# Thirteen more short fills on VectorE at the beginning of a channel-attention kernel

## The chip, the cores and the metric

The kernel runs on 1 core of one Trainium2 chip. Times are device microseconds of that core for one execution, medians of several executions. Before the change the time was 743.05 us (three runs, 742.87 to 743.95).

## The reference

The input `x` is one image of 384 x 384 positions with 384 channels (bf16); `w1` is 384 x 96, `w2` is 96 x 384.

```python
def reference(x, w1, w2):
    B, H, W, C = x.shape
    xf = x.reshape(B, H * W, C)
    gap = jnp.mean(xf, 1)                  # mean of every channel
    gmp = jnp.amax(xf, 1)                  # maximum of every channel
    h_a = gap @ w1;  h_a = h_a * (h_a > 0)
    h_m = gmp @ w1;  h_m = h_m * (h_m > 0)
    scale = _sigmoid(h_a @ w2 + h_m @ w2)
    return x * scale[:, None, None, :]     # (dtype casts cut)
```

No output can be written before all of `x` has been read once. The kernel keeps part of `x` and reads the rest a second time: the page shows 198.92 MB read, and `x` has 113.25 MB.

## The kernel before

There are three stages. (1) All rows are loaded; TensorE sums them with a vector of ones, VectorE keeps a running maximum in `acc` (11 rows per partition). (2) A short serial stretch, called *the gate* below: the maximum is folded to one row, transposed, reduced, passed through the two small matrices and the sigmoid. (3) Every row is multiplied by the scale and stored, while the rows that had to be dropped are loaded again.

Setup, which the change touches:

```python
    small = consts.tile([P, 16], BF16)
    ones_bf = small[:, 0:1]
    # ... cut: other views of `small`; none of them covers column 9
    nc.vector.memset(ones_bf, 1.0)
    pick = small[0:NQP, 10:10 + 2 * CQ].bitcast(F32)
    nc.vector.memset(pick, 0.0)
    for q in range(CQ):                                   # CQ = 3
        nc.vector.memset(pick[q * QP:q * QP + 1, q:q + 1], 1.0)
    # ... cut
    nc.vector.memset(bank_a, 0.0)                         # 128 x 512 f32 in PSUM
```

`bank_a` is a tile that the program places in PSUM; in the trace TensorE's 900 matmuls of the sums write it (L143, `bank_a<-x,small`).

The load loop of stage 1 and the fold at the start of the gate (line numbers in the profile: copy into `acc` L179, maximum L183, fold L203, reduce L214, multiply L226):

```python
    for i, (first, n, s, lo, hi) in enumerate(loads):
        rows = slots[s][:, lo:hi, :]
        # ... cut
        nc.sync.dma_start(out=rows[:, a:b, :], in_=...)   # the first load in two parts
        # ... cut: sums on TensorE
        if i == 0:
            nc.vector.tensor_copy(out=acc, in_=rows[:, 0:A, :])
        for j in range(0 if i else A, m, A):
            nc.vector.tensor_tensor(out=acc[:, 0:k, :], in0=acc[:, 0:k, :], in1=rows[:, j:j + k, :], op=ALU.max)
        # ... cut: two copies that keep rows in PSUM
    # ... cut
    while n > 1:                                          # fold, n starts at A = 11
        h = n // 2
        nc.vector.tensor_tensor(out=acc[:, 0:h, :], in0=acc[:, 0:h, :], in1=acc[:, n - h:n, :], op=ALU.max)
        n -= h
```

A tile scheduler decides the order in which each engine gets its instructions, so an instruction need not stand where the program has it (the fill of L115 starts at 1.00 us, those of L95 at 1.48 us).

## Time and profile before

| what | before |
|---|---|
| time, median | 743.05 us |
| moved by DMA | 312.32 MB, 421 GB/s over the span |
| VectorE (DVE) busy | 489.4 us, 66% of the span |
| VectorE idle ahead of its first copy | 5.44 us |
| gate, first fold step to first multiply | 5.50 us |

The page of the kernel before: span, busy time by engine, the DMA's busy share in 40 slices of the span in tenths, GB/s in the same slices, and the two queues that carry instructions (packets, MB, share of 16 engines).

```profile
span 741.5 us, 2477 instructions
PE 127.2 (17%) x966; PEld 40.6 (5%) x966; DVE 489.4 (66%) x168; ACT 3.3 (0%) x9; POOL 0.7 (0%) x6
DMA  9999999999999969999999999999999999999997
GB/s 383 423 435 434 433 430 418 428 429 426 427 422 422 418 254 378 402 435 446 432 431 428 432 437 436 436 432 432 427 434 437 436 436 432 432 427 432 441 437 340
q8 instruction: 7, 0.11, 0.1%
q14 instruction: 4, 0.03, 0.0%
```

The DMA's share is 1.01 from 7.1 to 262 us, 1.00 from 277 to 704 us, and 0.49 in the gate (271.4 to 276.9 us).

The timeline of VectorE at the beginning, before. Columns: start, duration in us, engine, line, operation, output<-input, shapes, count, and in brackets the idle time just before and what ended it.

```profile
0.81 0.06 DVE L89 MEMSET small<- 128x1 bf16 x1 [0.81 <-PEq L302]
0.84 0.06 DVE L93 MEMSET small<- 65x3 f32 x1
1.00 0.48 DVE L115 MEMSET bank_a<- 128x512 f32 x1
1.48 0.27 DVE L95 MEMSET small<- 1x1 f32 x3
7.18 1.26 DVE L179 COPY acc<-x_79 128x4224 bf16<-128x4224 bf16 x1 [5.44 <-DMA x_79<-in_x_dram]
...
25.49 9.53 DVE L183 TENSOR_TENSOR acc<-acc,x_84 128x4224 bf16<-128x4224 bf16 x4 [4.22 <-DMA x_84<-in_x_dram]
...
57.02 9.54 DVE L183 TENSOR_TENSOR acc<-acc,x_81 128x4224 bf16<-128x4224 bf16 x4 [0.48 <-DMA x_81<-in_x_dram]
```

The last fill ends at 1.75 us; then VectorE has nothing to do until the first load has landed. It also waits for later loads: 4.22 us at 25 us, 1.96 us at 47 us, some 0.5 us each for nine others before 134 us. Those waits after the first copy add up to 10.6 us. From 134 to 259 us it works without a gap.

The same view of the gate, before:

```profile
271.43 2.74 DVE L203 TENSOR_TENSOR acc<-acc 128x1920 bf16<-128x1920 bf16 x4
274.73 0.43 DVE L214 TENSOR_REDUCE small<-bank_a 128x2 bf16<-128x256 bf16 x1 [0.56 <-PE bank_b L213]
275.07 0.28 DVE L214 TENSOR_REDUCE small<-bank_b 128x1 bf16<-128x128 bf16 x1
275.61 0.16 DVE L219 SCALAR_TENSOR_TENSOR small<-bank_a,small 96x1 bf16<-96x1 f32 x1 [0.25 <-PE bank_a L218]
276.93 1.50 DVE L226 TENSOR_TENSOR x_79<-x_79,scale_bc 128x384 bf16<-128x384 bf16 x3 [1.17 <-ACT scale_bc L221]
```

Here every step waits for the one before, on VectorE, TensorE or ScalarE, while the DMA moves 124 GB/s, against 428 from 7.1 to 262 us.

### The profile page before, as it was taken

The page shows a single profiled execution, that of the slowest core. Times are in us where ns is not written, and L with a number is a line of the kernel's source. Part 1 is how long each engine was busy: PE and PEld are TensorE (multiplying, and loading weights), DVE is VectorE, ACT ScalarE, POOL GpSimd, SP SyncE. Part 2 cuts the span into 40 slices and gives each one's busy share as a digit, 9 for nine tenths or more (in the row PEclk, how much of TensorE's full clock was granted, in tenths as well). Part 3 has the DMA queues.
Part 4 walks back from the last instruction along what each step waited for, and adds up shares of the span by engine and source line. Part 5 has one row for each costly group of instructions (what it writes and reads, how often), then busy time and mean ns, then how long its engine had stood idle before and what let it go on. Part 6 is the DMA issues. An engine that isn't in the chain of part 4 may idle for free.

```text
span 741.5 us, 2477 instructions
## 1 busy us (share of the span) xinstructions
PE 127.2 (17%) x966; PEld 40.6 (5%) x966; DVE 489.4 (66%) x168; ACT 3.3 (0%) x9; POOL 0.7 (0%) x6
## 2 busy tenths in 40 slices
PE   3345443445454550000000000000000000000000
PEld 0011111111111120000000000000000000000000
DVE  6789999999999989999444443444444444444600
ACT  0000000000000000000000000000000000000000
POOL 0000000000000000000000000000000000000000
PEclk9865666655555555555555555555555555555555
DMA  9999999999999969999999999999999999999997
GB/s 383 423 435 434 433 430 418 428 429 426 427 422 422 418 254 378 402 435 446 432 431 428 432 437 436 436 432 432 427 434 437 436 436 432 432 427 432 441 437 340
DMA packets 18379, 312.32 MB, mean 421 GB/s; under 512 B 2400, under 2 KB 3008, under 8 KB 6592
## 3 DMA queue, kind: packets, MB, share of 16 engines
q1 hardware_dynamic: 12032, 198.92, 63.2%
q10 hardware_dynamic: 6336, 113.25, 35.7%
q8 instruction: 7, 0.11, 0.1%
q14 instruction: 4, 0.03, 0.0%
HBM read 198.92 MB, written 113.25 MB: 421 GB/s over the span
## 4 chain that ended last, share of the span: by engine, by line
another core or an unknown queue 44%; DMA 34%; DVE 14%; DVEq 1%; SPq 1%; issue 1%; PE 0%; ACT 0%; ACTq 0%
DMA x_81<-in_x_dram 9%; DMA x_82<-in_x_dram 7%; DVE acc L183 7%; DMA out_dram<-x_83 6%; DMA x_79<-in_x_dram 6%; DMA x_80<-in_x_dram 3%; DMA x_83<-in_x_dram 3%; DVE x_81 L226 1%; DVE x_80 L226 1%; DVE x_83 L226 1%; DVE x_82 L226 1%; DVE x_79 L226 1%; DVEq L313 1%; SPq L253 1%
## 5 line engine op out<-in xcount | busy, mean ns | idle before, releaser
L226 DVE TENSOR_TENSOR x_79<-x_79,scale_bc 128x16896 bf16<-128x16896 bf16 (+6 forms) x13 | 45.4, 3538 | 34.2 <-DMA x_79<-in_x_dram 33.0
L226 DVE TENSOR_TENSOR x_80<-x_80,scale_bc 128x16896 bf16<-128x16896 bf16 (+4 forms) x9 | 40.9, 4576 | 28.7 <-DMA x_80<-in_x_dram 28.7
L226 DVE TENSOR_TENSOR x_84<-x_84,scale_bc 128x16896 bf16<-128x16896 bf16 x4 | 35.8, 8958 | 33.1 <-DMA x_84<-in_x_dram 33.1
L226 DVE TENSOR_TENSOR x_83<-x_83,scale_bc 128x16896 bf16<-128x16896 bf16 x4 | 35.8, 8956 | 33.0 <-DMA x_83<-in_x_dram 33.0
L226 DVE TENSOR_TENSOR x_82<-x_82,scale_bc 128x16896 bf16<-128x16896 bf16 x4 | 35.8, 8957 | 32.8 <-DMA x_82<-in_x_dram 32.8
L226 DVE TENSOR_TENSOR x_81<-x_81,scale_bc 128x16896 bf16<-128x16896 bf16 (+3 forms) x6 | 36.0, 6021 | 31.0 <-DMA x_81<-in_x_dram 31.0
L183 DVE TENSOR_TENSOR acc<-acc,x_84 128x4224 bf16<-128x4224 bf16 (+3 forms) x21 | 47.3, 2253 | 5.4 <-DMA x_84<-in_x_dram 4.7
L143 PEld LDWEIGHTS <-small 128*1 128x1 bf16 x900 | 36.4, 110 | 229.9 <-issue 227.0
L183 DVE TENSOR_TENSOR acc<-acc,x_83 128x4224 bf16<-128x4224 bf16 (+1 forms) x19 | 42.8, 2253 | 1.3 <-DMA x_83<-in_x_dram 0.7
L183 DVE TENSOR_TENSOR acc<-acc,x_80 128x4224 bf16<-128x4224 bf16 (+1 forms) x18 | 40.6, 2257 | 3.0 <-DMA x_80<-in_x_dram 2.4
L183 DVE TENSOR_TENSOR acc<-acc,x_79 128x4224 bf16<-128x4224 bf16 (+1 forms) x17 | 38.9, 2287 | 1.5 <-DMA x_79<-in_x_dram 1.0
L183 DVE TENSOR_TENSOR acc<-acc,x_81 128x4224 bf16<-128x4224 bf16 (+2 forms) x17 | 37.9, 2229 | 1.5 <-DMA x_81<-in_x_dram 1.0
L183 DVE TENSOR_TENSOR acc<-acc,x_82 128x4224 bf16<-128x4224 bf16 x16 | 37.7, 2358 | 1.5 <-DMA x_82<-in_x_dram 1.0
L143 PE MATMUL bank_a<-x_84,small 128*1 128x512 bf16 (+2 forms) x165 | 21.6, 558 | 27.1 <-DMA x_84<-in_x_dram 27.1
L143 PE MATMUL bank_a<-x_79,small 128*1 128x512 bf16 (+1 forms) x150 | 20.4, 574 | 28.7 <-DMA x_79<-in_x_dram 28.7
L143 PE MATMUL bank_a<-x_80,small 128*1 128x512 bf16 (+3 forms) x150 | 21.0, 585 | 23.6 <-DMA x_80<-in_x_dram 23.6
L143 PE MATMUL bank_a<-x_83,small 128*1 128x512 bf16 (+2 forms) x159 | 20.3, 540 | 23.3 <-DMA x_83<-in_x_dram 23.3
L143 PE MATMUL bank_a<-x_82,small 128*1 128x512 bf16 (+2 forms) x138 | 19.6, 594 | 20.9 <-DMA x_82<-in_x_dram 20.9
L143 PE MATMUL bank_a<-x_81,small 128*1 128x512 bf16 (+3 forms) x138 | 19.4, 593 | 21.1 <-DMA x_81<-in_x_dram 21.1
L179 DVE COPY acc<-x_79 128x4224 bf16<-128x4224 bf16 x1 | 1.3, 1260 | 5.4 <-DMA x_79<-in_x_dram 5.4
L185 DVE COPY kept_ps<-x_79 128x3072 uint32<-128x3072 uint32 x1 | 3.4, 3354 | 0.0
L226 DVE TENSOR_TENSOR x_81<-kept_ps,scale_bc 128x6144 bf16<-128x6144 bf16 x1 | 3.4, 3350 | 0.0
(39 smaller groups left out, 22.5 us busy)
## 6 DMA issues: line engine op xcount, KB each, us to landing
x_84<-in_x_dram SPq DMA_DIRECT2D x5, 4224.0 KB, 27.4
x_79<-in_x_dram SPq DMA_DIRECT2D x5, 4224.0 KB, 27.4
x_80<-in_x_dram SPq DMA_DIRECT2D x5, 4224.0 KB, 27.7
x_81<-in_x_dram SPq DMA_DIRECT2D x5, 4224.0 KB, 27.4
x_82<-in_x_dram SPq DMA_DIRECT2D x5, 4224.0 KB, 27.4
x_83<-in_x_dram SPq DMA_DIRECT2D x4, 4224.0 KB, 27.4
out_dram<-x_82 ACTq DMA_DIRECT2D x4, 4224.0 KB, 74.3
out_dram<-x_83 ACTq DMA_DIRECT2D x4, 4224.0 KB, 71.1
```

The source lines that it names most:

```text
L143: nc.tensor.matmul(sum_ps[q * QP:q * QP + 1, 0:g * P], lhsT=ones_bf[:, 0:1], rhs=rows[:, k:k + g, q * P:(q + 1) * P], start=(done + k == 0 ...
L179: nc.vector.tensor_copy(out=acc, in_=rows[:, 0:A, :])
L183: nc.vector.tensor_tensor(out=acc[:, 0:k, :], in0=acc[:, 0:k, :], in1=rows[:, j:j + k, :], op=ALU.max)
L185: nc.vector.tensor_copy(out=kept_ps.bitcast(U32), in_=rows.bitcast(U32))
L226: nc.vector.tensor_tensor(out=dst, in0=src, in1=scale_bc.unsqueeze(1).to_broadcast([P, n, C]), op=ALU.mult)
L253: nc.sync.dma_start(out=slots[s][:, j:j + m, :], in_=rows_of(xr, first, n)[:, j:j + m, :])
L313: with _tile.TileContext(nc) as tc:
```

## The change

It adds thirteen fills of one bf16 element to VectorE's work at the beginning. They write an element that nothing reads. The intent is to see what a dozen very short instructions cost at this place.

```diff
+SHORT_FILLS = 13
@@
     for q in range(CQ):
         nc.vector.memset(pick[q * QP:q * QP + 1, q:q + 1], 1.0)
+    for _ in range(SHORT_FILLS):
+        nc.vector.memset(small[0:1, 9:10], 0.0)
```

## The prediction

> What bounds the kernel now. It is bound by DMA traffic. The page shows 312.32 MB moved in a span of 741.5 us (421 GB/s), and its row of slices shows the DMA share at 9 tenths in every slice but one: slice 15 (about 260 to 278 us), where the last loads end, the maximum is folded and the gate computed, at 254 GB/s. Busy time by stretch agrees: DMA share 1.01 from 7 to 262 us, 0.63 to 277, 1.00 to 704. VectorE is busy 489.4 us (66%) and sets the pace alone only in that gate stretch and for some of 134 to 271 us.
>
> What the change adds. Thirteen fills of one bf16 element, nothing else. The built streams of the other four engines are the same. On VectorE one fill falls before the 128x512 fill of the PSUM bank and twelve after the last of the three 1x1 fills of `pick`; each waits for the one before it. The existing 1x1 fills take 59 ns and start about 0.1 us apart (three of them in 0.27 us, by the timeline). Thirteen cost, as an estimate from that, 1.2 to 1.6 us of VectorE.
>
> How much of it is on the critical path: none. By the timeline VectorE ends its fills at 1.74 us and then stands idle 5.44 us for the first load (copy into `acc` at 7.18 us, released by the DMA). With the change the fills should end near 3.0 us, 4 us before that load lands. TensorE's first matmul waits for the bank fill, which moves by at most 0.1 us to about 1.6 us; it starts at 4.42 us, released by its own load.
>
> One second-order effect: later VectorE instructions stand 13 places further back in its instruction stream. [...] The page agrees that there are block fetches in the run: 7 packets of about 16 KB on one instruction queue and 4 of about 8 KB on another. A VectorE boundary could move from a place where work was queued up into the serial gate stretch (271 to 277 us), where a hiccup is exposed. I estimate that at 0 to 0.4 us, from one otherwise unexplained pause of 0.36 us at an issue on the load queue near 221 us.
>
> Predicted time: 743.3 us, 80% range 741.8 to 745.5 (before: 742.87 to 743.95). Chances: faster by over 2% 0.01, within 2% 0.97, slower by over 2% 0.02.
>
> What would show each step right: VectorE has 13 more instructions and about 0.8 us more busy time; the copy into `acc` still starts near 7.2 us, released by the DMA, with its idle time cut from 5.4 to about 4.2 us; the first matmul near 4.4 us; the gate sequence (fold, transposes, reduce, sigmoid) still about 5.5 us from 271.4 us; the span near 741.7 us. Wrong: the copy starting later than 7.3 us with a VectorE release; a new idle time on VectorE within the gate stretch or between maxima without a DMA behind it.
>
> What would make it wrong: an instruction fetch that stalls VectorE for microseconds[...] and now falls where the next instruction is needed at once; or a load and store order that tips over with the small shift and costs a transfer slot (a full 44-row load takes about 10 us).

Two passages are cut from it: a sentence on how instructions are fetched, and the reason given for the feared stall. The forecast came to 743.3 us, against 743.05 before, with 0 to 0.4 us for a boundary, an estimate from the pause of 0.36 us in the trace. That a boundary could move into the gate and show there was my guess at this point; the runs below found 0.37 us of it in the gate with sixteen fills and none with thirteen, and the longest pause of this kind that they found was about 0.4 us.

## The result, and the profile after

The changed kernel took 743.9 us (four runs, 743.27 to 744.15), the kernel before beside it 743.02 us (742.87 to 743.95). The ratio is 1.0007, 95% interval 0.9993 to 1.0021: the same. All ratios here are the mean time of one kernel's fast runs over that of the other's of the same rounds, so they are not quite the ratio of the medians quoted.

The page after, in the same lines:

```profile
span 742.0 us, 2490 instructions
PE 131.0 (18%) x966; PEld 41.2 (6%) x966; DVE 490.1 (66%) x181; ACT 3.3 (0%) x9; POOL 0.7 (0%) x6
DMA  9999999999999979999999999999999999999997
GB/s 378 424 433 437 429 434 418 429 424 428 429 419 421 420 253 377 419 429 431 437 434 434 435 437 421 430 435 435 437 435 435 426 430 432 435 437 429 436 430 341
```

There are 13 instructions and 0.7 us more on VectorE. The DMA's rates are nearly the same, and the lines of the two instruction queues are the same word for word.

The timeline of VectorE at the beginning, after (the names of the slots are now all shown as `x`, and lines stand 2 or 4 further down; L99 are the new fills):

```profile
0.86 0.06 DVE L99 MEMSET small<- 1x1 bf16 x1
1.02 0.48 DVE L119 MEMSET bank_a<- 128x512 f32 x1
1.50 0.27 DVE L97 MEMSET small<- 1x1 f32 x3
1.83 1.33 DVE L99 MEMSET small<- 1x1 bf16 x12
8.29 1.26 DVE L183 COPY acc<-x 128x4224 bf16<-128x4224 bf16 x1 [5.13 <-DMA x<-in_x_dram]
```

The fills are over at 3.16 us. Each takes 59 ns and starts 116 ns after the one before. They all write the same element, and in the built program each waits on a semaphore for the one before it; the second and the third fill of this profile (0.83 and 0.86 us) wait for no other, and start 0.02 to 0.03 us after the one before. So the 116 ns are those of a chain; what independent fills would cost was not measured. VectorE then still waits 5.13 us for the load. But the copy starts 1.1 us later than in the other profile, released by the DMA. Is that chance, or do the fills hold up the load? The first two experiments ask this.

The gate, after:

```profile
271.64 2.74 DVE L207 TENSOR_TENSOR acc<-acc 128x1920 bf16<-128x1920 bf16 x4
274.93 0.43 DVE L218 TENSOR_REDUCE small<-bank_a 128x2 bf16<-128x256 bf16 x1 [0.56 <-PE bank_b L217]
275.27 0.28 DVE L218 TENSOR_REDUCE small<-bank_b 128x1 bf16<-128x128 bf16 x1
275.81 0.16 DVE L223 SCALAR_TENSOR_TENSOR small<-bank_a,small 96x1 bf16<-96x1 f32 x1 [0.25 <-PE bank_a L222]
277.14 1.50 DVE L230 TENSOR_TENSOR x<-x,scale_bc 128x384 bf16<-128x384 bf16 x3 [1.17 <-ACT scale_bc L225]
```

It begins 0.21 us later and is, wait for wait, as long as before: 277.14 - 271.64 = 5.50 us.

### The profile page after: what moved, and what is told of

It reads as the page before. It is cut to its first block, busy times and chain, and to the rows that moved or that the text cites. A ratio compares the mean times of both kernels' runs of the same rounds, so it can differ in the third digit from the quotient of the medians.

```text
span 742.0 us, 2490 instructions
## 1 busy us (share of the span) xinstructions
PE 131.0 (18%) x966; PEld 41.2 (6%) x966; DVE 490.1 (66%) x181; ACT 3.3 (0%) x9; POOL 0.7 (0%) x6
## 4 chain that ended last, share of the span: by engine, by line
another core or an unknown queue 46%; DMA 34%; DVE 9%; PE 3%; SPq 1%; DVEq 1%; issue 1%; ACT 0%; ACTq 0%
DMA x<-in_x_dram 28%; DMA out_dram<-x 6%; DVE x L230 6%; PE bank_a L147 3%; DVE acc L187 2%; DVEq L317 1%; SPq L257 1%; DVE kept_ps L189 0%; DVE acc L207 0%; SPq L174 0%; DVE acc L230 0%; DVE acc L183 0%; PE bank_a L224 0%; ACT scale_bc L225 0%
## 5 line engine op out<-in xcount | busy, mean ns | idle before, releaser
L230 DVE TENSOR_TENSOR x<-x,scale_bc 128x16896 bf16<-128x16896 bf16 (+11 forms) x40 | 229.1, 5768 | 193.0 <-DMA x<-in_x_dram 191.9
L187 DVE TENSOR_TENSOR acc<-acc,x 128x4224 bf16<-128x4224 bf16 (+4 forms) x108 | 245.3, 2271 | 13.2 <-DMA x<-in_x_dram 9.8
L147 PE MATMUL bank_a<-x,small 128*1 128x512 bf16 (+2 forms) x900 | 126.0, 587 | 141.1 <-DMA x<-in_x_dram 141.0
L189 DVE COPY kept_ps<-x 128x3072 uint32<-128x3072 uint32 x1 | 3.4, 3354 | 0.0
L230 DVE TENSOR_TENSOR x<-kept_ps,scale_bc 128x6144 bf16<-128x6144 bf16 x1 | 3.4, 3350 | 0.0
L207 DVE TENSOR_TENSOR acc<-acc 128x384 bf16<-128x384 bf16 (+2 forms) x4 | 2.6, 659 | 0.1
L230 DVE TENSOR_TENSOR acc<-acc,scale_bc 128x1920 bf16<-128x1920 bf16 (+1 forms) x2 | 2.4, 1250 | 0.0
L164 PEld LDWEIGHTS <-x 128*128 128x128 bf16 x48 | 1.5, 108 | 0.0
L99 DVE MEMSET small<- 1x1 bf16 x13 | 0.8, 59 | 0.7
```

The source lines that it names most:

```text
L99: nc.vector.memset(small[0:1, 9:10], 0.0)
L147: nc.tensor.matmul(sum_ps[q * QP:q * QP + 1, 0:g * P], lhsT=ones_bf[:, 0:1], rhs=rows[:, k:k + g, q * P:(q + 1) * P], start=(done + k == 0 ...
L164: nc.tensor.matmul(gsum_ps[:, q:q + 1], lhsT=rows[:, k, q * P:(q + 1) * P], rhs=ones_bf, start=False, stop=(last and k == n - 1 and q == C ...
L189: nc.vector.tensor_copy(out=kept_ps.bitcast(U32), in_=rows.bitcast(U32))
L230: nc.vector.tensor_tensor(out=dst, in0=src, in1=scale_bc.unsqueeze(1).to_broadcast([P, n, C]), op=ALU.mult)
```

## The experiments

The theory (A): the fills lie in a wait of VectorE, and even beyond that wait there is slack; the time doesn't change. The rivals: (B) the fills hold up the first load and the 0.9 us between the medians is real; (C) such fills cost nothing anywhere, so that this place is not special; (D) instruction fetch never shows in the time of VectorE, against the prediction's guess that it may cost up to 0.4 us in the gate.

### The kernel before against itself, and the changed one again

No edit. Five rounds each, on one chip, with the same nine runs of the kernel before (median 743.35, 742.03 to 744.48).

> The kernel before, unchanged, timed against itself, to see the spread. Theory A (the fills are hidden in VectorE's wait for the first load; the 0.9 us between the two medians, 743.02 and 743.9, is spread): ratio 1.000 within 0.1% either way, and in a second profile the first copy into acc starts anywhere from 7.2 to 8.3 us[...]. Theory B (the 0.9 us is a cost of the fills: they delay the landing of the first load by about 1.1 us): the copy starts near 7.2 us again and no run of this kernel reaches the 743.9 us of the changed one more than now and then.

> The changed kernel, unchanged, in five rounds against the kernel before on one chip. Theory A: ratio 1.000 within 0.1%, the interval contains 1; the first copy starts anywhere from 7.2 to 8.3 us, always released by the DMA, never by a fill (fills over at about 3.2 us). Theory B: ratio 1.001 to 1.0015 with an interval clear of 1, and the copy starts near 8.3 us again.

Measured: again_before 743.2 us (742.44 to 743.3), ratio 1.000, interval 0.9987 to 1.0012. again_after 743.2 us (742.64 to 743.47), ratio 1.000, interval 0.9986 to 1.0014. The first copy in the two profiles, again_before first:

```profile
8.22 1.26 DVE L179 COPY acc<-x 128x4224 bf16<-128x4224 bf16 x1 [6.48 <-DMA x<-in_x_dram]
```

```profile
7.33 1.26 DVE L183 COPY acc<-x 128x4224 bf16<-128x4224 bf16 x1 [4.17 <-DMA x<-in_x_dram]
```

This time the kernel without the fills has the late copy and the one with them the early one. The landing times in the trace show why: a load reports 16 times. In again_before 15 of the 16 reports of the second part had come by 6.93 us and the last came at 8.12 us; in the first profile of the changed kernel it was 7.27 and 8.19 us. One late share of 16 holds up the copy, in some executions, with or without fills. So theory B falls: the late landing is not the fills' doing, and two of the nine runs of the kernel before, 743.89 and 744.48 us, are about as long as the 743.9 us of the first comparison or longer. Its 0.9 us are spread, as far as can be seen; the interval by itself would still admit a cost of 1.0 us. (The expectations had said up to 0.1% either way; the intervals are a little wider than that.)

### The same thirteen fills in the gate

The diffs of the experiments are shortened, and are against the changed kernel.

```diff
-    for _ in range(SHORT_FILLS):
-        nc.vector.memset(small[0:1, 9:10], 0.0)
@@
+    fold = ctx.enter_context(ExitStack())
+    fold.enter_context(tc.manual_schedule(engines={mybir.EngineType.DVE}))
     while n > 1:
         h = n // 2
         nc.vector.tensor_tensor(...)
+        for _ in range(SHORT_FILLS if n == A else 0):
+            nc.vector.memset(small[0:1, 9:10], 0.0)
         n -= h
```

The fills come once, after the first of the four fold steps. The added context, closed after the loop, holds VectorE to the program's order; built without it, the program has all thirteen fills ahead of the first copy. With it, the built order of all other instructions is that of the kernel before.

> The same thirteen fills, each waiting for the one before, but none at the beginning: all of them between the first and the second step of the fold of acc, in the stretch where VectorE alone sets the pace and the DMA is not saturated. Both theories agree that VectorE is exposed here; from the 0.116 us from start to start measured at the beginning, the second fold step should start about 1.4 to 1.5 us later after the first one than in the kernel before (where it is 1.19 us), and the sigmoid and the first multiply the same 1.4 us later. Time: up to +1.4 us, ratio 1.001 to 1.002, unless the saturated stage behind absorbs it. This shows what the fills cost where they are not hidden, and that five rounds can see a microsecond. Theory C (thirteen small fills cost nothing anywhere): ratio 1.000 and no later sigmoid.

Measured: 744.5 us (743.98 to 744.69), ratio 1.0018, interval 1.0006 to 1.0031. The gate in its timeline:

```profile
271.26 1.16 DVE L207 TENSOR_TENSOR acc<-acc 128x1920 bf16<-128x1920 bf16 x1
272.36 1.35 DVE L209 MEMSET small<- 1x1 bf16 x12
273.76 0.75 DVE L207 TENSOR_TENSOR acc<-acc 128x1152 bf16<-128x1152 bf16 x1
...
278.06 1.49 DVE L233 TENSOR_TENSOR x<-x,scale_bc 128x384 bf16<-128x384 bf16 x3 [1.17 <-ACT scale_bc L228]
```

The second fold step starts 2.50 us after the first, against 1.19 us before, and the first multiply comes 6.80 us after the start of the fold, against 5.50. The same instructions that cost nothing at the beginning cost 1.3 us here. (That is 0.1 us under the expectation: the first fill overlaps the end of the fold step and the last runs beside the next one.) Of it 1.15 us arrive in the medians, 744.5 against 743.35; by the interval it is 0.4 to 2.3 us. Theory C falls.

### A hundred fills at the beginning

```diff
-SHORT_FILLS = 13
+SHORT_FILLS = 100
@@ and VectorE's work of the load loop ordered behind the last fill
     for _ in range(SHORT_FILLS):
-        nc.vector.memset(small[0:1, 9:10], 0.0)
+        last_fill = nc.vector.memset(small[0:1, 9:10], 0.0)
@@
+    behind = ctx.enter_context(ExitStack())
+    behind.enter_context(tc.issue_after(last_fill.ins))
     for i, (first, n, s, lo, hi) in enumerate(loads):
```

The ordering is closed after the loop, and it is needed. Without it, the scheduler put only 35 of 50 fills ahead of the first copy and spread the others into later places.

> One hundred fills in place of thirteen, and everything VectorE does with the loads ordered behind the last one. At 0.116 us each they end near 13.4 us, which is 6 us after the first load has landed, so the first copy is now released by a fill and starts about 6 us late. Theory A, with slack: in the kernel before VectorE still waits for loads for 10.6 us in sum after its first copy and before 134 us, and four loads are in flight until 25.4 us, so the delay is caught up and the time is +0 to +1 us (ratio 1.000 to 1.0015). Theory B or any theory in which the start of VectorE is on the critical path: +6 us or more (ratio 1.008 and up); if each fill counts in full, +11.6 us (1.016).

Measured: 743.75 us (743.18 to 744.91), ratio 1.0012, interval 0.9999 to 1.0026.

```profile
1.82 11.40 DVE L99 MEMSET small<- 1x1 bf16 x99
13.23 1.26 DVE L185 COPY acc<-x 128x4224 bf16<-128x4224 bf16 x1
...
46.79 9.54 DVE L189 TENSOR_TENSOR acc<-acc,x 128x4224 bf16<-128x4224 bf16 x4 [0.33 <-DMA x<-in_x_dram]
56.82 9.54 DVE L189 TENSOR_TENSOR acc<-acc,x 128x4224 bf16<-128x4224 bf16 x4 [0.49 <-DMA x<-in_x_dram]
...
271.60 2.74 DVE L210 TENSOR_TENSOR acc<-acc 128x1920 bf16<-128x1920 bf16 x4
```

The copy starts 6 us late and has no wait for the load any more. The waits at 25, 35 and 47 us shrink to 0.33 us in sum, and at 56.82 us VectorE stands where it stood before (57.02). The fold starts at 271.60, against 271.43. So at the fold 6 us of pure delay are swallowed, whereas 13 fills are 1.4 us of work in a wait. In the time a small cost can't be told from none: the interval reaches from 0 to +1.9 us.

### A hundred and fifty, and two hundred

Only the number changes.

> One hundred and fifty fills, ordered ahead of all the work on the loads. At 0.1157 us each, as measured with one hundred, they end near 19.1 us, so the first copy starts 12 us later than in the kernel before (7.18 us). Theory A says that only what exceeds the 10.6 us of later waits for loads is paid: +1 to +2.5 us, ratio 1.0015 to 1.0035. VectorE should have almost no wait for a load left before 134 us. If the slack were unlimited: 0; if every fill counted: +17 us (1.023).

> Two hundred fills, ending near 24.9 us, 17.7 us after the first copy of the kernel before. Theory A: 17.7 less the 10.6 us of slack is +7 us; besides, the first four loads have landed by 25.4 us and no slot is free before about 30.5 us, so the DMA stands idle there for some 7 us, which may add up to 3 us: +7 to +10 us, ratio 1.0095 to 1.0135. The fold of acc then starts near 278.5 to 281 us. If every fill counted: +23 us (1.031).

Measured, against 742.22 us before: 150 fills 751.23 us (749.03 to 752.82), ratio 1.0112, interval 1.0087 to 1.0138; 200 fills 750.91 us (750.2 to 751.65), ratio 1.0117, interval 1.0101 to 1.0132. Two hundred lies in the expected range, but 150 costs as much as 200, where +1 to +2.5 us was expected: a miss. Its timeline:

```profile
19.02 1.26 DVE L185 COPY acc<-x 128x4224 bf16<-128x4224 bf16 x1
...
46.57 9.54 DVE L189 TENSOR_TENSOR acc<-acc,x 128x4224 bf16<-128x4224 bf16 x4 [3.90 <-DMA x<-in_x_dram]
57.27 220.54 DVE L189 TENSOR_TENSOR acc<-acc,x 128x4224 bf16<-128x4224 bf16 x94 [1.17 <-DMA x<-in_x_dram]
277.85 2.74 DVE L210 TENSOR_TENSOR acc<-acc 128x1920 bf16<-128x1920 bf16 x4
```

VectorE starts late and nevertheless waits 3.90 and 1.17 us for loads. The built load queues tell why: in both kernels the scheduler, seeing VectorE late, had put the load of the slot that the kernel before calls `x_81`, which waits for nothing, ahead of the reloads of `x_79` and `x_80`, which VectorE reads first. The experiment had changed two things. With 200 fills this didn't hurt VectorE, which was later still and worked without a gap from 24.80 us to the fold at 278.64 us; and for the same reason the 7 us of idle DMA that I had expected there did not come (from 25.5 to 31 us it moved 386 GB/s and more, and from 25.5 to 46.5 us its share was 1.01). The range was hit, with one of its two terms wrong, which is partly luck: the fold is 7.2 us later than before, and where the other 1.5 of the 8.7 us between the medians lie is not shown. With 150 fills the fold is 6.4 us later; the rest of its 9.0 us comes after the gate, and why is open.

### A hundred and fifty with the loads in the old order

```diff
     behind.enter_context(tc.issue_after(last_fill.ins))
+    behind.enter_context(tc.manual_schedule(engines={mybir.EngineType.SP}))
```

> The 150 fills again, but with the loads held in the order that the kernel before has. In the first run of 150 fills the scheduler had put the sixth load (for the slot that VectorE reads last) ahead of the two that VectorE needed next, and VectorE stood idle 3.9 and 1.2 us for them. Theory A with that explanation: those two waits go, VectorE is busy almost without a gap from 19.0 us on, the fold starts near 19.0 + 253.8 = 272.9 us (253.8 us is what the same work took without a gap in the run of 200 fills) against 277.85, and the time is +1.4 to +3 us on the kernel before (ratio 1.002 to 1.004). If 150 fills are dear by themselves, as the first run would have it: +9 us again (1.012), fold at 277.8 us.

Measured: 745.05 us (744.56 to 745.75) against 743.24, ratio 1.0028, interval 1.0014 to 1.0042.

```profile
19.01 1.26 DVE L186 COPY acc<-x 128x4224 bf16<-128x4224 bf16 x1
...
271.53 1.76 DVE L190 TENSOR_TENSOR acc<-acc,x 128x3072 bf16<-128x3072 bf16 x1 [0.36 <-DVE acc L190]
273.33 2.74 DVE L211 TENSOR_TENSOR acc<-acc 128x1920 bf16<-128x1920 bf16 x4
```

With the loads in order 150 fills cost +1.8 us, and the fold starts 1.9 us later than before. That is the 11.8 us by which the copy is late (19.01 - 7.18) less the 10.6 us of later waits, which would be 1.2, plus the 0.36 us in the first line after the dots, to which the next experiments return. The remaining 0.3 us fit the step of about 0.035 us that stands between two maxima even without a wait: eleven waits that go leave eleven such steps, as an estimate 0.4 us. (The one wait that is left, 0.17 us near 261 us, is there in the kernel before too.) So the slack is a little less than the 10.6 us of waits, about 10.3 us here and, with 200 fills, 17.6 us late less 7.2 us paid, 10.4 us; beyond it a fill is paid.

### Fifteen, sixteen, seventeen and twenty: the instruction fetch

The trace's packet records hold four packets of 8 KB on the second instruction queue within the span of the kernel before, at 111.2, 224.3, 280.7 and 376.8 us. After the change they are at 91.1, 224.6, 277.2 and 376.7 us. Only the first and the third moved with VectorE's instruction count, by 20.1 and 3.5 us, so I take them for fetches of VectorE's instructions. Thirteen fills had carried the third from the multiplies to the end of the gate. A few more fills, I expected, would carry it further into the gate. Every kernel here is the one of a hundred fills with another number, one look each.

> Sixteen fills: three more than the change, so that VectorE's instruction-block boundary, which thirteen fills moved from about 280.7 us to about 277 us (second fetch of 8 KB after 250 us), moves a few instructions further into the serial stretch of fold, reduce and gate. Theory A with the second-order effect of the prediction: a pause of up to 0.4 us may show in one of the gaps there (0.56 us before the first reduce, 0.25 before the fused add, 1.17 before the first multiply). Theory D (instruction fetch never shows): those gaps stay within 0.03 us. Time not told apart by one run: 742 to 745 us.

> Twenty fills, the boundary another four instructions earlier, into the fold steps or the reduces. Same alternatives as with sixteen: up to 0.4 us in one of the gaps of the serial stretch (35 ns between the fold steps, 0.56, 0.25 and 1.17 us after them), or no change of any of them by more than 0.03 us. One run: 742 to 745 us.

> Sixteen fills once more, to see whether the pause of 0.37 us that stood before the first reduce of the gate (0.41 us after the semaphore instruction ahead of it, where the other kernels have 0.04 us) comes back. If it is the block boundary, which by this lies between the 191st and the 192nd traced instruction of VectorE in every kernel: the same 0.4 us at the same place. If it was chance: 0.04 us.

> Fifteen fills: the boundary then lies between the two reduces of the gate. The pause starts when the first reduce is handed on and runs beside it; the second starts 0.34 us after the first, so at most 0.05 us shows: second reduce 0.34 to 0.40 us after the first, 0.04 us before the first reduce. By chance or any other cause: no difference between fifteen and sixteen.

> Seventeen fills: the boundary lies between the last fold step and the semaphore instruction that waits about 0.9 us for TensorE's transposes, so the pause is hidden in that wait: 0.04 us before the first reduce, all gaps of the gate as in the kernel before. By chance or any other cause: as with sixteen.

Measured, one run each: 743.26 (16), 743.67 (20), 748.81 (16 again), 744.13 (15), 743.01 (17) us. The first reduce with 16 fills, with 16 again, and with 17:

```profile
274.95 0.43 DVE L221 TENSOR_REDUCE small<-bank_a 128x2 bf16<-128x256 bf16 x1 [0.93 <-PE bank_b L220]
```

```profile
275.61 0.43 DVE L221 TENSOR_REDUCE small<-bank_a 128x2 bf16<-128x256 bf16 x1 [0.93 <-PE bank_b L220]
```

```profile
274.58 0.43 DVE L221 TENSOR_REDUCE small<-bank_a 128x2 bf16<-128x256 bf16 x1 [0.56 <-PE bank_b L220]
```

The profile puts the idle time down to TensorE in all three. But in the trace the semaphore instruction that waits for TensorE is over at the same time after the fold's end in each; what follows it after 0.04 us in the others comes after 0.41 us with sixteen, both times. With fifteen the second reduce starts 0.41 us after the first instead of 0.34 (a little over what was expected). With seventeen and with twenty nothing in the gate moved. This pattern is what a pause of about 0.37 us makes that sits between the 191st and the 192nd traced instruction of VectorE, whatever those are: with sixteen they are the semaphore instruction and the reduce behind it, with fifteen the two reduces, with seventeen a fold step and the semaphore instruction, which comes 0.85 us after the start of the fold step anyway, because it waits for TensorE. The 0.36 us in the run of 150 fills in the old order is the same pause further on: it stands between the 319th and the 320th instruction, 128 later, again right behind a semaphore instruction.

The changed kernel itself has the pause 128 instructions earlier, between its 63rd and 64th instruction, which its timeline shows only as a longer wait for a load. Before and after:

```profile
87.11 9.54 DVE L183 TENSOR_TENSOR acc<-acc,x_84 128x4224 bf16<-128x4224 bf16 x4 [0.49 <-DMA x_84<-in_x_dram]
```

```profile
87.73 19.16 DVE L187 TENSOR_TENSOR acc<-acc,x 128x4224 bf16<-128x4224 bf16 x8 [1.16 <-DMA x<-in_x_dram]
```

The load landed 0.23 us later than before, and the maximum starts 0.44 us after the semaphore instruction that waits for it, against 0.05 us before; in again_after it is 0.45 us. The next wait for a load, 0.47 us at 97 us before, is gone: slack has absorbed the pause.

Theory D falls: a pause that moves with the instruction count shows in VectorE's time, and thirteen fills put one where it costs nothing, while in the gate theirs lies in the wait for ScalarE. That the pause belongs to a block boundary is my inference from this count and from the 8 KB packets; no trace shows it. It is not a wait for the packet seen beside it: that packet starts 1.3 to 3.6 us after the pause is over in all five cases. What VectorE's sequencer does meanwhile is open. The pause on the load queue near 221 us, from which the prediction took its 0.4 us, stands at the same instruction of that queue in all fourteen profiles, and one of the two 8 KB packets that did not move follows it by 3.1 to 3.4 us.

Not explained is the single time of 748.81 us. Its gate is like that of the first run of the same kernel (first multiply 5.87 us after the fold's start in both). Of the rest, 0.7 us are there at the fold already and the others come in stage 3, where a block took about 20.2 us in it and 20.0 in the other, with the same instructions. It is one run; nothing rests on it.

## Why the prediction was right

- *The kernel is bound by the DMA; VectorE has a wait at the beginning.* Right: 13 and even 100 fills leave the time the same within the noise, the same 13 in the gate cost 1.15 us of the median. (The DMA's share is below nine tenths in two slices, not one; the prediction overlooked the last.)
- *The fills cost 1.2 to 1.6 us of VectorE and end near 3.0 us.* They end at 3.16 us, 1.4 us later than the last fill of before; busy time rose by 0.7 us, not 0.8.
- *The copy still starts near 7.2 us, with 4.2 us of idle time.* Not so in the first profile (8.29 us, 5.13 us idle). This check was badly put: the landing moves between 6.9 and 8.4 us from run to run, in kernels with few fills or none. What ended the wait, the DMA, was as predicted, and that is what the check should have named.
- *TensorE's first matmul is not moved.* The bank fill moved from 1.00 to 1.02 us, long before any load lands. The first matmul started at 4.63 us, against 4.42, because its load landed at 4.49 us instead of 4.28; in again_before and again_after it was 4.28 and 4.56 us.
- *The gate stays 5.5 us.* 5.50 us in both profiles.
- *A block boundary may land in the gate, 0 to 0.4 us.* By the count (191st to 192nd instruction) it did land there, ahead of the first multiply, where the wait for ScalarE hides it: the cost is 0. With sixteen it is 0.37 us; both ends of the estimate exist. That thirteen lie on the cheap side is luck as far as the prediction goes, which could not place the boundary. One of its signs of being wrong, new idle time between maxima without a DMA behind it, did appear in part: about 0.4 us at 87 us, from another boundary. It cost nothing, since it fell where VectorE had slack.
- *743.3 us, 741.8 to 745.5.* 743.9 in the first comparison, 743.2 in the second. How near the median came says little, since the times of one kernel spread by 1 us and more.

On size: a fill took 59 ns for 1x1 and for 128x1 and 61 ns for 65x3, so hardly anything of these depends on it, and 485 ns for the 128x512 f32 fill into PSUM. On the pause: in the gate it was hidden with 13, 17 and 20 fills and exposed by 0.37 us with 16, and at 87 us it was exposed by about 0.4 us with 13.

## What to carry to other kernels

Before costing an added instruction, look at what ends the idle time behind its place: where a transfer did here, thirteen fills, 1.4 us of work in a wait of 5.44 us, were free (ratio 1.0007), and the later waits of the same engine for transfers were slack on top, here about 10.4 us. The same instructions between two dependent steps were paid in full, 1.3 us. When an experiment adds work, compare the built order of all queues with the kernel before: here 150 fills cost 9.0 us with one load moved forward and 1.8 us without.

## What else the traces show

- If the two packets that moved are VectorE's, its fetches here are of 8 KB. The pauses that were found lie 128 instructions apart (63rd to 64th, 191st to 192nd and 319th to 320th). 7 packets of 16 KB are seen on the other instruction queue.
- An exposed pause was about 0.35 to 0.4 us (for example 0.41 against 0.04 us), in five profiles right behind an instruction in which VectorE's sequencer waits for a semaphore; with fifteen fills 0.07 us of it showed between two reduces, and a chain of short fills ran over the same places in the count without a pause (200 fills, 116 ns from start to start throughout).
- The last of a load's 16 shares came 0.8 to 1.2 us after the other fifteen in four of the fourteen profiles, and in three of them moved the first copy from about 7 to between 8.2 and 8.4 us.
